# Fused attention and MLP on one Trainium2 core: one ScalarE Mish instruction in place of the exp, min, product, ln, exp chain

## The chip, the core and the metric

The kernel runs on one NeuronCore of a Trainium2 chip. A core has engines that run side by side and meet at semaphores: TensorE (PE, matrix multiply; its weight loads are listed as PEld), VectorE (DVE), ScalarE (ACT), GpSimd (POOL) and SyncE (SP, which issues most of the transfers). The metric is device time of one execution in microseconds (us). A lower time is better.

## What is computed

A relative-position attention whose output, laid out as 2304 tokens of 512 features, goes through an MLP with the Mish activation g = h * tanh(ln(1 + exp(h))). The first half is attention over 4 batches, 8 heads, 576 positions and 64 features a head, with a bias that a small network makes from the positions. The second half is where the change lies:

```python
def _moe_ref(x, w_in, w_out):          # x 2304 x 512, w_in 512 x 2048, w_out 2048 x 512
    h = x @ w_in
    sp = np.where(h > 20.0, h, np.log1p(np.exp(np.minimum(h, 20.0))))
    g = h * np.tanh(sp)
    return (g @ w_out).astype(np.float32)
```

## The kernel before

The program has three stages. The first (to about 60 us) makes the position bias and writes it out to memory (`evac`, L500 to L514). The second (to about 310 us) is attention: a software pipeline over 80 steps (`step`, L389), in which step n issues the scores of n, the exponentials of n, the transposes of n-2 on TensorE with their copies out of PSUM on ScalarE (L287, L290, L295, L296), and products with v (L313, L317). The last four steps, called with NS to NS+3, issue no exponentials any more: only transposes, copies and products.

The third stage is the MLP. The tokens are cut into five blocks (four of 512 and one of 256), and each block's hidden features into groups, which makes 72 units of one 128x512 tile each: 16 units for a block of 512 tokens, 8 for the block of 256. Every product is made of three fp32r matmuls (high x high, high x low, low x high parts) in order to keep fp32 accuracy, so a unit costs TensorE 12 matmuls of 512 columns in `hidden` (L581) and 12 in `project` (L615). In the block of 256 tokens `hidden` issues 24 of 256 columns instead.

The order of work is written by hand: each engine executes its instructions in the order of the program. In the loop at L669, round k issues `hidden` of unit k, `project` of unit k-3, and `gate` of unit k-1. So TensorE has two other unit-steps between the hidden product of a unit and its projection, plus one more of each kind. `hidden` writes h into one of four PSUM tiles. The rest of the activation is spread over two functions:

- `hidden`, after its matmuls: e = Exp(h) on ScalarE (L594), a minimum with E20 on VectorE (L595), and (e+2)*e on VectorE (L596). h stays in PSUM.
- `gate`: r = Ln(e+2) (L604) and r = Exp(-r) (L605) on ScalarE, which together make 1/(e+2); e = h*e (L606) and e = e*r (L607) on VectorE; then two splits of weights into high and low parts as long as any are left (`split_weights`, L130: a ScalarE copy at L135 and a VectorE subtraction at L136); then the split of the result: the high part as a ScalarE copy (L611) and the low part as a VectorE subtraction (L612).

`split_x` (L563) does the same for the next block's tokens (L570, L571, L573). The constant `two`, a tile of 128x96 of which one column is read, is the bias of the Ln. It is the first tile of the first pool on the left side of SBUF. At L49 the table set with both exp and ln is loaded on ScalarE before anything else. The units 0, 1 and 2 are begun between the attention's last steps (L652 to L660), so that the two stages overlap.

Of the kernel before, what the change touches and what calls it, by code (L numbers as in the profile page):

```python
# [7 lines left out]
F32 = mybir.dt.float32  # L8
F32R = mybir.dt.float32r
U32 = mybir.dt.uint32  # L10
AF = mybir.ActivationFunctionType
ALU = mybir.AluOpType
# [5 lines left out]
DM, DFF = 512, 2048  # L18
NT = B * S
P = 128  # L20
# [3 lines left out]
PAD = 16  # L24
PITCH = S + 2 * PAD
BIG = 3.0e38
E20 = 485165195.40979


ORDER = [0, 1, 4, 2, 3]  # L30
TB = 512
# [13 lines left out]
def kernel(ctx: ExitStack, tc, qk, v, wb, w2, w_in, w_out, psia, psi4, rinv, eye, out):  # L45
    nc = tc.nc
    pe, dve, act, pool, sp = nc.tensor, nc.vector, nc.scalar, nc.gpsimd, nc.sync
# [15 lines left out]
    const = sbuf("const")  # L63
# [4 lines left out]
    dram = ctx.enter_context(tc.tile_pool(name="dram", bufs=1, space=DRAM))  # L68


    two = const.tile([P, 96], F32, name="two")
    ident = const.tile([P, P], F32, name="ident")

    bias_d = [dram.tile([H, (P if c < 4 else 64) * PITCH + 2 * PAD], F32, name=f"bias_d{c}") for c in range(5)]
# [55 lines left out]
    def split_weights(eng):  # L130
        job, c = w32.pop(0)
        if job not in w_hi:
            w_hi[job] = ring.tile([P, 512], F32R, name="wh{}{}{}".format(*job))
            w_lo[job] = ring.tile([P, 512], F32R, name="wl{}{}{}".format(*job))
        act.copy(w_hi[job], c)  # L135
        eng.tensor_tensor(w_lo[job], c, w_hi[job].bitcast(F32), op=ALU.subtract)  # L136
# [317 lines left out]
    act.dma_start(out=psi4_t, in_=psi4)  # L454
    sp.dma_start(out=w2t, in_=w2)
    act.dma_start(out=rinv_t, in_=rinv)
    dve.memset(two, 2.0)
    dve.tensor_scalar(bb, psi4_t, wbt[:, 1:2], None, op0=ALU.mult)
    dve.tensor_scalar(at, at, wbt[:, 0:1], None, op0=ALU.mult)
    ts = [t for c in ORDER for t in range(8 * c, min(8 * c + 8, S // 16))]  # L460
    bps_t, h_t = {}, {}
# [14 lines left out]
    for idx, t in enumerate(ts):  # L476
# [4 lines left out]
        for cg in (3, 2, 1, 0):  # L481
            e = min(price, key=lambda k: spent[k] + price[k])
# [75 lines left out]
    mp = sbuf("mp", 2, side="right")  # L558
# [18 lines left out]
    h_t, gs, ys = {}, {}, {}  # L577
# [3 lines left out]
    def hidden(blk, fs):  # L581
        n = blocks[blk][1]
        h = h_ps.tile([P, TB], F32, name="h")
        for u, f in enumerate(fs):
            g4, r = divmod(f, 4)
            k = 0
            for w, x in ((w_hi, x_hi[blk]), (w_lo, x_hi[blk]), (w_hi, x_lo[blk])):
                for d in range(HP):
                    pe.matmul(h[:, u * n:(u + 1) * n], w["i", g4, d][:, r * P:(r + 1) * P], x[:, d, :n],  # L589
                              start=(k == 0), stop=(k == 11))  # L590
                    k += 1

        e = mp.tile([P, TB], F32, name="e", bufs=3)
        act.activation(e, h, AF.Exp)  # L594
        dve.tensor_scalar(e, e, E20, None, op0=ALU.min)  # L595
        dve.scalar_tensor_tensor(e, e, 2.0, e, op0=ALU.add, op1=ALU.mult)  # L596
        h_t[blk, fs] = (h, e)

    def gate(blk, fs, splits=0):
        r = mp.tile([P, TB], F32, name="r")  # L600
        ghi = mp.tile([P, TB], F32R, name="ghi")
        glo = mp.tile([P, TB], F32R, name="glo")
        h, e = h_t.pop((blk, fs))
        act.activation(r, e, AF.Ln, bias=two[:, 0:1])  # L604
        act.activation(r, r, AF.Exp, scale=-1.0)  # L605
        dve.tensor_tensor(e, h, e, op=ALU.mult)  # L606
        dve.tensor_tensor(e, e, r, op=ALU.mult)  # L607
        for _ in range(splits):
            if w32:
                split_weights(dve)  # L610
        act.copy(ghi, e)  # L611
        dve.tensor_tensor(glo, e, ghi.bitcast(F32), op=ALU.subtract)  # L612
        gs[blk, fs] = (ghi, glo)

    def project(blk, fs):  # L615
        t0, n = blocks[blk]
        ghi, glo = gs.pop((blk, fs))
        nt = n // P
        if fs[0] == 0:
            ys[blk] = [y_ps.tile([P, DM], F32, name=f"y{t}") for t in range(nt)]  # L620
        for t in range(nt):
            for u, f in enumerate(fs):
                g4, r = divmod(f, 4)
                whi, wlo = w_hi["o", g4, r], w_lo["o", g4, r]
                c0 = u * n + t * P
                for k, (g, w) in enumerate(((ghi, whi), (ghi, wlo), (glo, whi))):
                    pe.matmul(ys[blk][t], g[:, c0:c0 + P], w,  # L627
                              start=(f == 0 and k == 0), stop=(f == NFC - 1 and k == 2))
        if fs[-1] == NFC - 1:
            for t in range(nt):  # L630

                if t % 2 == 0:
                    yo = convp.tile([P, 512, 2], U32, name="w64").bitcast(F32).rearrange("p f t -> p (f t)")
                part = yo[:, t % 2 * DM:(t % 2 + 1) * DM]
                rows = out[t0 + t * P:t0 + (t + 1) * P, :]
                if blk == len(blocks) - 1 and t == nt - 1:

                    dve.tensor_copy(part[:, :DM // 2], ys[blk][t][:, :DM // 2])
                    rest = mp.tile([P, TB], F32, name="r")[:, :DM // 2]
                    act.copy(rest, ys[blk][t][:, DM // 2:])  # L640
                    sp.dma_start(out=rows[:, :DM // 2], in_=part[:, :DM // 2])
                    act.dma_start(out=rows[:, DM // 2:], in_=rest)
                    continue
                if t % 2:
                    act.copy(part, ys[blk][t])
                else:
                    dve.tensor_copy(part, ys[blk][t])
                sp.dma_start(out=rows, in_=part)
            del ys[blk]


    hidden(*units[0])  # L652
    step(NS)
    gate(*units[0])
    hidden(*units[1])
    step(NS + 1)
    gate(*units[1])
    hidden(*units[2])
    step(NS + 2)
    step(NS + 3)  # L660
# [8 lines left out]
    for k in range(2, len(units) + LAG2):  # L669
        if k < len(units):  # L670
            blk, fs = units[k]
            f = fs[0]
            if blk + 1 < len(blocks):
                early = 2 * (len(fs) - 1)
                if f == 6 - 2 * early:
                    load_x(blk + 1, xp)
                    x_lo[blk + 1] = (xa if blk % 2 else xp).tile([P, HP, TB], F32R, name="xlo")
                    load_r(blk + 1, x_lo[blk + 1].bitcast(F32), 0, HP)

                if f >= 8 - early:  # L680
                    split_x(blk + 1, XPARTS[f - 8 + early:f - 8 + early + len(fs)])
            if k > 2:
                hidden(blk, fs)
        if k >= LAG2:
            project(*units[k - LAG2])
        if 2 <= k - 1 < len(units):
            gate(*units[k - 1], 2)
# [54 lines left out]
```

## Time and profile before

| | us |
|---|---|
| median of three runs | 701.82 (701.07 to 703.33) |
| span of the profiled execution | 700.9 |
| TensorE matmul busy | 672.9 (96%) |
| VectorE busy | 517.3 (74%) |
| ScalarE busy | 458.4 (65%) |
| GpSimd busy | 72.4 (10%) |
| mean granted TensorE clock | 0.994 of full speed |

The page cuts the span into 40 slices. TensorE shows a 9 in tenths in every slice from the seventh to the last but one. VectorE and ScalarE fall from 8 and 9 in the attention to 5 to 7 and 4 to 5 in the MLP. A share of busy time is a mean over stages with different limits, so the views below are read stage by stage. A row of the chain of waits says at which time which piece of work held the end of the program; a row of the waits says who waited for whom.

### The profile page before, as it was taken

The page shows a single profiled execution, that of the slowest core. Times are in us where ns is not written, and L with a number is a line of the kernel's source. Part 1 is how long each engine was busy: PE and PEld are TensorE (multiplying, and loading weights), DVE is VectorE, ACT ScalarE, POOL GpSimd, SP SyncE. Part 2 cuts the span into 40 slices and gives each one's busy share as a digit, 9 for nine tenths or more (in the row PEclk, how much of TensorE's full clock was granted, in tenths as well). Part 3 has the DMA queues.
Part 4 walks back from the last instruction along what each step waited for, and adds up shares of the span by engine and source line. Part 5 has one row for each costly group of instructions (what it writes and reads, how often), then busy time and mean ns, then how long its engine had stood idle before and what let it go on. Part 6 is the DMA issues. An engine that isn't in the chain of part 4 may idle for free.

```text
span 700.9 us, 13630 instructions
## 1 busy us (share of the span) xinstructions
PE 672.9 (96%) x5156; PEld 511.2 (73%) x5156; DVE 517.3 (74%) x1082; ACT 458.4 (65%) x987; POOL 72.4 (10%) x85
## 2 busy tenths in 40 slices
PE   5878999999999999999999999999999999999997
PEld 2224666776777666668888888889988888888886
DVE  7995898888988878868788566655775567665554
ACT  6895988888899888876675544444554455454443
POOL 0000142322222222710000000000000000000000
PEclk9999999999999999999999999999999999999999
DMA  4997688787778767204000120023005000010001
GB/s 150 318 285 228 195 273 263 216 284 225 245 234 266 241 231 240 55 22 116 1 1 0 66 56 1 1 76 106 1 1 150 1 1 0 1 60 1 1 0 60
DMA packets 46081, 81.88 MB, mean 117 GB/s; under 512 B 14400, under 2 KB 23104, under 8 KB 46016
## 3 DMA queue, kind: packets, MB, share of 16 engines
q1 hardware_dynamic: 43568, 72.70, 32.8%
q0 software_dynamic: 1872, 8.09, 3.9%
q8 instruction: 40, 0.66, 0.4%
q10 hardware_dynamic: 576, 0.22, 0.1%
q14 instruction: 25, 0.20, 0.1%
HBM read 60.60 MB, written 20.40 MB: 116 GB/s over the span
## 4 chain that ended last, share of the span: by engine, by line
PE 71%; ACT 9%; DVE 7%; DMA 3%; issue 2%; DVEq 0%; ACTq 0%
PE h L589 28%; PE y L627 28%; PE o L313 5%; PE s L220 5%; ACT pt L252 5%; DVE pt L237 4%; ACT main L295 3%; PE tp L287 3%; PE tp L290 1%; DMA w<-in_w_in_dram 1%; DMA w<-in_w_out_dram 1%; PE o L317 1%; DVE w L123 1%; DVE x L320 1%; DVE w L125 1%
## 5 line engine op out<-in xcount | busy, mean ns | idle before, releaser
L252 ACT ACTIVATE pt<-pt,m 128x576 f32<-128x576 f32 x144 | 112.2, 780 | 33.5 <-DVE m L237 32.9
L627 PE MATMUL y<-who,ghi 128*128 128x512 f32 x288 | 112.1, 389 | 0.0
L627 PE MATMUL y<-wlo,ghi 128*128 128x512 f32 x288 | 112.1, 389 | 0.0
L627 PE MATMUL y<-who,glo 128*128 128x512 f32 x288 | 112.0, 389 | 0.0
L611 ACT CAST ghi<-e 128x512 fp32r<-128x512 f32 x72 | 44.7, 621 | 93.5 <-DVE e L607 93.5
L237 DVE CUSTOM_DVE_ANT_0 pt<-s,bias 128x576 f32<-128x576 f32 (+1 forms) x112 | 81.3, 753 | 17.8 <-PE s L220 16.6
L594 ACT ACTIVATE e<-h 128x512 f32<-128x512 f32 x72 | 43.0, 597 | 65.9 <-PE h L589 65.7
L595 DVE TENSOR_SCALAR e<-e 128x512 f32<-128x512 f32 x72 | 30.6, 426 | 74.0 <-ACT e L594 74.0
L612 DVE TENSOR_TENSOR glo<-e,ghi 128x512 fp32r<-128x512 f32 x72 | 49.8, 692 | 44.9 <-ACT ghi L611 44.9
L589 PE MATMUL h<-xhi,whi 128*128 128x512 f32 (+1 forms) x320 | 79.1, 369 | 0.0
L589 PE MATMUL h<-xhi,wli 128*128 128x512 f32 (+1 forms) x320 | 78.7, 368 | 0.0
L589 PE MATMUL h<-xlo,whi 128*128 128x512 f32 (+1 forms) x320 | 78.7, 368 | 0.0
L313 PE MATMUL o<-main,vt 128*64 128x320 f32 (+1 forms) x512 | 73.8, 411 | 3.1 <-DVE x L320 3.0
L295 ACT COPY main<-tp 128x512 f32<-128x512 f32 x126 | 66.5, 577 | 2.0 <-DMA bias_d<-bt 1.9
L287 PE MATMUL tp<-ident,pt 64*128 64x64 f32 x1184 | 61.7, 227 | 6.3 <-ACT main L295 4.7
L589 PEld LDWEIGHTS h<-xhi,whi 128*128 128x128 f32 x320 | 57.1, 188 | 11.7 <-issue 0.7
L287 PEld LDWEIGHTS tp<-ident,pt 64*128 64x128 f32 x1184 | 53.5, 139 | 15.2 <-ACT main L295 13.1
L589 PEld LDWEIGHTS h<-xhi,wli 128*128 128x128 f32 x320 | 56.9, 189 | 10.0
L589 PEld LDWEIGHTS h<-xlo,whi 128*128 128x128 f32 x320 | 56.9, 189 | 10.0
L627 PEld LDWEIGHTS y<-who,glo 128*128 128x128 f32 x288 | 54.1, 188 | 11.3
L627 PEld LDWEIGHTS y<-who,ghi 128*128 128x128 f32 x288 | 54.1, 188 | 11.0
L627 PEld LDWEIGHTS y<-wlo,ghi 128*128 128x128 f32 x288 | 54.1, 188 | 10.9
(69 smaller groups left out, 1126.9 us busy)
## 6 DMA issues: line engine op xcount, KB each, us to landing
bias_d<-bt SPq DMA_DIRECT2D x36, 295.5 KB
w<-in_w_in_dram SPq DMA_DIRECT2D x16, 512.0 KB
w<-in_w_out_dram SPq DMA_DIRECT2D x16, 512.0 KB
qkhi<-in_qk_dram POOLq DMA_DIRECT2D x13, 608.0 KB, 4.5
rawqk<-in_qk_dram SPq DMA_DIRECT2D x13, 608.0 KB
vt<-in_v_dram SPq DMA_DIRECT2D x16, 320.0 KB
out_dram<-w SPq DMA_DIRECT2D x17, 256.0 KB
x_d<-x SPq DMA_DIRECT2D x32, 128.0 KB
```

The source lines that it names most:

```text
L220: pe.matmul(s[:, j, :SH], q[rows, c * P:(c + 1) * P], k[rows, KO + j * SH:KO + (j + 1) * SH], start=(t == 0), stop=(t == len(terms) - 1))
L237: dve.tensor_tensor_reduce(out=halves(pt[rows, sl]), in0=s[rows, :, :SH], in1=halves(bt[rows, sl]), scale=-0.125, scalar=BIG, op0=ALU.add, ...
L252: act.activation(ps, ps, AF.Exp, bias=m[:, u:u + 1], scale=-1.0, accum_out=sums[i][:, k:k + 1])
L287: pe.transpose(tp[:, k * 64:k * 64 + 64], pt[rows, c0:c0 + P], ident[rows, rows])
L295: copy(main[:, :, :, q0:q0 + 64], tp.rearrange("p (h k q) -> p h k q", h=2, k=4))
L313: pe.matmul(o[h * 64:h * 64 + 64, :w], vt[:, h, k, :], main[:, h, k, :], start=(k == 0), stop=False, **kw)
L589: pe.matmul(h[:, u * n:(u + 1) * n], w["i", g4, d][:, r * P:(r + 1) * P], x[:, d, :n], start=(k == 0), stop=(k == 11))
L594: act.activation(e, h, AF.Exp)
L595: dve.tensor_scalar(e, e, E20, None, op0=ALU.min)
L611: act.copy(ghi, e)
L612: dve.tensor_tensor(glo, e, ghi.bitcast(F32), op=ALU.subtract)
L627: pe.matmul(ys[blk][t], g[:, c0:c0 + P], w, start=(f == 0 and k == 0), stop=(f == NFC - 1 and k == 2))
```

## The change

`hidden` ends with its matmuls. `gate` has one ScalarE instruction with the Mish function, which reads h from PSUM and writes g to SBUF, and then the splits as before. The tile e (three buffers) and the constant `two` with its memset are gone; r (two buffers) is now called g. The preload at L49 is left as it is.

```diff
-    two = const.tile([P, 96], F32, name="two")
...
-    dve.memset(two, 2.0)
...
-        e = mp.tile([P, TB], F32, name="e", bufs=3)
-        act.activation(e, h, AF.Exp)
-        dve.tensor_scalar(e, e, E20, None, op0=ALU.min)
-        dve.scalar_tensor_tensor(e, e, 2.0, e, op0=ALU.add, op1=ALU.mult)
-        h_t[blk, fs] = (h, e)
+        h_t[blk, fs] = h
 
     def gate(blk, fs, splits=0):
-        r = mp.tile([P, TB], F32, name="r")
+        g = mp.tile([P, TB], F32, name="g")
         ghi = mp.tile([P, TB], F32R, name="ghi")
         glo = mp.tile([P, TB], F32R, name="glo")
-        h, e = h_t.pop((blk, fs))
-        act.activation(r, e, AF.Ln, bias=two[:, 0:1])
-        act.activation(r, r, AF.Exp, scale=-1.0)
-        dve.tensor_tensor(e, h, e, op=ALU.mult)
-        dve.tensor_tensor(e, e, r, op=ALU.mult)
+        act.activation(g, h_t.pop((blk, fs)), AF.Mish)
         for _ in range(splits):
             if w32:
                 split_weights(dve)
-        act.copy(ghi, e)
-        dve.tensor_tensor(glo, e, ghi.bitcast(F32), op=ALU.subtract)
+        act.copy(ghi, g)
+        dve.tensor_tensor(glo, g, ghi.bitcast(F32), op=ALU.subtract)
         gs[blk, fs] = (ghi, glo)
...
-                    rest = mp.tile([P, TB], F32, name="r")[:, :DM // 2]
+                    rest = mp.tile([P, TB], F32, name="g")[:, :DM // 2]
```

## Rows read from the trace of the kernel before

**Rows 1.** Chain of waits, hand-over and MLP: start us, us, engine, tile, line, count

```profile
292.45 0.70 PE tp L287 x15
...
302.14 2.99 PE h L589 x12
...
314.88 2.72 PE y L627 x12
...
686.24 10.21 PE y L627 x45
```

**Rows 2.** Windows: span, then busy us (instructions) of PE PEld DVE ACT POOL, clock, DMA

```profile
40.00:60.00 20.00, 15.41 (x150) 5.61 (x144) 16.45 (x43) 14.82 (x36) 0.18 (x2) 0.98 0.91 284
340.00:360.00 20.00, 20.00 (x90) 16.57 (x89) 16.02 (x27) 12.62 (x22) 0.00 (x0) 1.00 0.00 0
```

**Rows 3.** Waits of PE from 285 to 372 us: total us, times, longest

```profile
PE tp L287 <- ACT main L295: 0.4, 2, 0.2
```

**Rows 4.** Lines by form, 340 us on: count | busy us, mean ns | idle before, releaser

```profile
L604 ACT ACTIVATE r<-e,two 128x512 f32<-128x512 f32 x65 | 46.5, 715 | 0.0
L607 DVE TENSOR_TENSOR e<-e,r 128x512 f32<-128x512 f32 x65 | 45.0, 692 | 7.1 <-DVE e L606 0.5
L606 DVE TENSOR_TENSOR e<-h,e 128x512 f32<-128x512 f32 x65 | 44.4, 684 | 4.5 <-ACT r L604 4.5
L596 DVE SCALAR_TENSOR_TENSOR e<-e 128x512 f32<-128x512 f32 x64 | 44.3, 693 | 2.2
L605 ACT ACTIVATE r<-r 128x512 f32<-128x512 f32 x65 | 41.3, 635 | 2.1
L611 ACT CAST ghi<-e 128x512 fp32r<-128x512 f32 x66 | 41.0, 621 | 89.5 <-DVE e L607 89.5
L594 ACT ACTIVATE e<-h 128x512 f32<-128x512 f32 x64 | 38.2, 597 | 58.0 <-PE h L589 57.8
L595 DVE TENSOR_SCALAR e<-e 128x512 f32<-128x512 f32 x64 | 27.2, 426 | 66.6 <-ACT e L594 66.6
...
L571 ACT CAST xhi<-xraw 128x512 fp32r<-128x512 f32 x12 | 7.4, 621 | 15.1 <-DVE xraw L570 15.1
...
L135 ACT CAST who<-w 128x512 fp32r<-128x512 f32 x8 | 4.6, 610 | 0.0
```

**Rows 5.** ACT timeline at the start: the table load before the first function

```profile
0.74 1.28 ACT L49 ACT_TABLE_LOAD   x1 [0.74 <-PEq L729]
```

**Rows 6.** ACT timeline at the hand-over: start us, us, line, operation [idle before]

```profile
301.47 0.28 ACT L296 COPY tail<-tp 128x128 f32<-128x128 f32 x1
...
305.16 0.60 ACT L594 ACTIVATE e<-h 128x512 f32<-128x512 f32 x1 [0.50 <-PE h L589]
305.81 1.08 ACT L295 COPY main<-tp 128x512 f32<-128x512 f32 x2
```

**Rows 7.** PE timeline at the hand-over

```profile
305.06 0.71 PE L287 MATMUL tp<-ident,pt 64*128 64x64 f32 x16
...
309.01 2.37 PE L313 MATMUL o<-main,vt 128*64 128x320 f32 x16
```

**Rows 8.** ACT timeline at the end

```profile
695.80 0.59 ACT L645 COPY w<-y 128x512 f32<-128x512 f32 x1 [2.77 <-PE y L627]
697.61 0.37 ACT L640 COPY r<-y 128x256 f32<-128x256 f32 x1 [1.23 <-DVE w L638]
```

**Rows 9.** DVE timeline at the end

```profile
695.12 0.69 DVE L647 COPY w<-y 128x512 f32<-128x512 f32 x1 [1.37 <-PE y L627]
```

**Rows 10.** PE timeline at the end

```profile
693.78 0.39 PE L627 MATMUL y<-wlo,ghi 128*128 128x512 f32 x1
...
695.14 0.39 PE L627 MATMUL y<-wlo,ghi 128*128 128x512 f32 x1
```

**Rows 11.** Chain of waits at the end of the bias stage

```profile
54.43 4.05 DMA bias_d<-bt
```

More of the change, by code (lines that the diff above doesn't have):

```diff
@@ L26 @@
 BIG = 3.0e38
-E20 = 485165195.40979
 ORDER = [0, 1, 4, 2, 3]
```

## The prediction, made before the changed kernel ran

> **What bounds the kernel now.** I read the chain of waits first, because it says which work held the end at each moment. From 292.45 us on every piece of it is TensorE's, one behind the other without a gap: transposes and products of the last attention steps, the first hidden products between them (the longest, 2.99 us), and from 314.88 us the steady pattern, in which a hidden product and a projection take 2.72 us each, 5.44 us a unit. The last piece, 10.21 us of projections, ends at 686.24 + 10.21 = 696.45 us [rows 1]. The windows say the same in another way: from 340 to 360 us TensorE is busy for 20.00 of 20.00 us at full granted clock, while VectorE has 16.02 and ScalarE 12.62 [rows 2]. The waits of TensorE itself settle it: between 285 and 372 us it waited 0.4 us in all, for copies of the attention's transposes, and for nothing that the activation makes [rows 3]. The two engines that the change relieves do wait, and a lot: the copy of the high part waits 89.5 us in all for the product before it, the first Exp 58.0 us for TensorE, the minimum 66.6 us for that Exp [rows 4]. These are waits of engines with time to spare.
>
> **What the change removes.** Per unit, from the rows of the steady stage [rows 4]: on VectorE 0.426 + 0.693 + 0.684 + 0.692 = 2.495 us (minimum, sum and product, two products), on ScalarE 0.597 + 0.715 + 0.635 = 1.947 us (Exp, Ln, Exp). Over 72 units that is 180 us of VectorE and 140 us of ScalarE. None of it lies on the path: TensorE doesn't wait for it. Worth at the end: 0. The memset of the constant at the start goes too; its result is first read by the Ln in the MLP, so this is 0 as well.
>
> **What it adds.** One ScalarE instruction per unit, of a function that the trace of before doesn't show. The nearest row is the Exp that reads the same h from PSUM in the same shape with no pointer operand, 0.597 us; the Ln with a pointer to its bias takes 0.715 us [rows 4]. I take 0.60 us. From the other side, I bound it by what ScalarE can hide: after the change a unit with everything in it has one high-part copy (0.621), two weight copies (2 x 0.610) and one token copy (0.621), 2.46 us, out of TensorE's 5.44 us; the Mish instruction could take 2.98 us, five times the Exp, before ScalarE became the bound [rows 1, 4]. With 0.60 us ScalarE needs 3.06 us of the 5.44, and most units, which have no weights or tokens left to split, 1.22 us. Cost: 0, between 0 and 0 up to five times the row.
>
> **One table load more.** The preload names a set with exp and ln. If Mish is in another, ScalarE has to load a table once, since after the attention's last Exp nothing but copies and Mish is left. The row of a load is 1.28 us [rows 5]. Behind it on ScalarE stand the first Mish, its copy, and the copies of the next transposes, for which TensorE's products wait. The cover: ScalarE ends the copies of step NS at 301.47 + 0.28 = 301.75 us. Load 1.28, Mish 0.60 and high-part copy 0.62 end at about 304.25 us. The next copies started at 305.81 us before, behind an Exp that itself waited for h (the change removes that Exp from here), and their transposes only start at 305.06 and last 0.71 us [rows 6, 7]. So about 1.5 us of cover is left in front of these copies, and behind them another 309.01 - 306.89 = 2.1 us until the products that read them [rows 6, 7]. A load of up to some 4.9 us would be free. Without the cover it would cost its own 1.28 us, once, 0.2%. Cost taken: 0, bounds 0 and 1.3 us.
>
> [...]
>
> **What moves.** ScalarE no longer waits for a new h in the middle of the round; it reads h one round later, in `gate`. So h stays in PSUM no longer than before, when the product h*e read it there in the same function: the four buffers suffice. The waits of the high-part copy for VectorE (89.5 us) go, and ScalarE waits for TensorE instead: nothing is late next, as the Mish of unit k-1 needs an h that is a round old. No transfer is issued in `hidden` or `gate`, so no queue is moved past.
>
> **The end.** Behind TensorE's last matmul stand VectorE's copies, ScalarE's copy at 697.61 us and the transfer of the result [rows 8]. None is touched but for the name of a tile. Cost 0.
>
> **Sum.** 700.9 us of span + 0 = 700.9 us. The median of the runs, 701.82 us, stands 0.9 us above the span; I carry this over and forecast 701.8 us. About 0.3%, 2.1 us, is what a measurement of this kernel can tell from no change; its own three runs spread over 2.3 us.
>
> **Rivals.**
>
> *TensorE was held back by the other engines all along.* [...] The end of the trace speaks against it: VectorE was idle for 1.37 us before 695.12 us and ScalarE for 2.77 us before 695.80 [rows 8, 9], and in that stretch six matmuls took 695.14 - 693.78 = 1.36 us [rows 10], 0.227 us each, the pace of the busy stretch to the digit. Chance 0.02. A small form of it: the four hidden products in the hand-over take up to 2.99 us instead of 2.72 [rows 1]; all of that back is at most 1.1 us, 700.7, inside the bound of no change.
>
> *The addresses move (slower, or faster).* The constant taken out is 384 bytes per partition at the head of the left side of SBUF; every tile of bias and attention on that side moves by as much. The one place where transfers hold the end for long is the write-out of the bias: the transfer engines are busy for 0.91 of 40 to 60 us [rows 2], and a piece of 4.05 us at 54.43 us is on the chain [rows 11]. If transfers from the new addresses are slower there, the piece grows; I price it at its own length, twice it or none: 705.9 us or 697.8. It decides from 2.1 us on, about 5% over the 40 us in which the bias is written out. No row shows a transfer at two alignments, so I can't exclude it. Chance 0.04 for each sign.
>
> [...]
>
> *The tables are swapped in every unit (slower).* If the copies of the MLP needed another set than Mish, each unit would have two loads: 2 x 1.28 + 0.60 + 0.62 = 3.8 us, or 5.0 us with the two weight copies, still under 5.44; only units with a token copy too reach 5.6 us [rows 1, 4, 5], which makes some 2 us over a dozen such units: 704 us. It hurts from 2.1 us a load on, (5.44 - 1.22) / 2; every 0.1 us above that costs 72 x 0.2 = 14 us. Against it: in the row of before the copies are COPY and CAST operations, not ACTIVATE, and run in one set beside Exp and Ln [rows 4]. Chance 0.04.
>
> [...]
>
> *The change doesn't do what it says:* Mish is made of several instructions. Up to 2.98 us a unit this gives the same time, 701.8. Chance 0.03, and it is counted as no change.
>
> **How the numbers follow.** The forecast has 0.83, with noise of a measurement 0.02 of that on either side outside 0.3%. Faster: 0.02 (contention) + 0.04 (addresses) + 0.02 (noise) = 0.08. Slower: 0.04 + 0.04 + 0.02 = 0.10, of which some of the table case is hidden: 0.08. No change: 0.84. The range takes the noise of the three runs on either side, and the bound of the table load, 1.3 us: 699.8 to 703.9 us. It leaves the address cases and the contention out, which hold about 0.1, and the far half of the table case.
>
> **What would show it.** Right: TensorE's pieces from 292 us on stand without a gap at 2.72 us; one more table load of about 1.3 us at about 300 to 302 us; Mish at about 0.60 us; VectorE's busy time about 180 us lower, ScalarE's about 97 us (140 - 72 x 0.60); the last matmul at about 696.5 us. Wrong: TensorE waiting for ghi, glo or a copy at L295 after 300 us, a matmul pace other than 0.227 us, table loads in more than one place, or the first score of the attention and the bias write-out ending more than 1 us away from before.

## The result, and the profile after

The changed kernel takes 710.13 us (median of four runs, 709.19 to 711.09) where the kernel before takes 701.93: a ratio of 1.0107, 95% interval 1.0083 to 1.0132. It is slower by 8.2 us. The forecast was no change at 701.8 us.

| | before | after |
|---|---|---|
| span of the profiled execution, us | 700.9 | 708.2 |
| TensorE busy, us | 672.9 | 681.8 |
| VectorE busy, us | 517.3 | 346.9 |
| ScalarE busy, us | 458.4 | 365.2 |
| mean granted TensorE clock | 0.994 | 0.993 |

The relief came as forecast: VectorE works 170 us less and ScalarE 93 us less. But TensorE, which has the same 5156 matmuls to do, is busy 8.9 us longer. The chain of waits of the changed kernel (start us, us, engine, tile, line, count) shows where; its rows answer to [rows 1]:

```profile
295.11 2.94 PE h L586 x12
...
315.86 2.80 PE h L586 x12
...
380.18 2.80 PE y L616 x12
382.98 2.73 PE h L586 x12
...
693.10 10.52 PE y L616 x45
```

There is still no gap in it, and 12 matmuls take 2.80 us instead of 2.72: 0.233 us a matmul instead of 0.227. In the kernel before, the first hidden product starts at

```profile
296.91 2.92 PE h L589 x12
```

and the last projection ends at 696.45 us [rows 1], 399.5 us later. After, it is from 295.11 to 693.10 + 10.52 = 703.62 us, 408.5 us. So the MLP takes 9.0 us more. It starts 1.8 us sooner, and what follows the last matmul takes 0.1 us more: 9.0 - 1.8 + 0.1 = 7.3 us of span. Of the remaining 0.9 us of the 8.2, 0.8 lies outside the span (709.94 us for the execution whose span is 708.2, 701.82 for 700.9), a part that ranges from 1.7 to 2.9 us within the runs of the first experiment below alone; so the experiments are compared by their ratios and by the length of the MLP.

The windows exclude a slower clock, and VectorE or ScalarE being short of time. The columns are those of [rows 2]; TensorE is busy 20.00 of 20.00 us at full granted clock, in 88 matmuls instead of 90, while VectorE and ScalarE are busy for no more than 3.37 and 3.98 us of the later stretch:

```profile
340.00:360.00 20.00, 20.00 (x88) 16.09 (x87) 9.10 (x15) 10.44 (x19) 0.00 (x0) 1.00 0.00 0
600.00:620.00 20.00, 20.00 (x88) 16.27 (x87) 3.37 (x5) 3.98 (x7) 0.00 (x0) 1.00 0.00 1
```

The lines by form from 340 us on answer to [rows 4]. The Mish instruction takes 593 ns, and ScalarE now runs so far ahead that the copy of the high part waits for TensorE to free its buffer:

```profile
L600 ACT CAST ghi<-g 128x512 fp32r<-128x512 f32 x65 | 40.4, 621 | 231.7 <-PE y L616 231.6
L596 ACT ACTIVATE g<-h 128x512 f32<-128x512 f32 x65 | 38.6, 593 | 0.0
```

And the ScalarE timeline at the hand-over shows the one table load, which answers to [rows 5, 6]:

```profile
299.69 0.28 ACT L294 COPY tail<-tp 128x128 f32<-128x128 f32 x1
299.99 1.28 ACT L596 ACT_TABLE_LOAD   x1
301.29 0.60 ACT L596 ACTIVATE g<-h 128x512 f32<-128x512 f32 x1
301.92 0.62 ACT L600 CAST ghi<-g 128x512 fp32r<-128x512 f32 x1
303.99 1.08 ACT L293 COPY main<-tp 128x512 f32<-128x512 f32 x2 [1.45 <-PE tp L285]
```

### The profile page after: what moved, and what is told of

Same layout as the page of the kernel before. It is cut to its first block, busy times and chain, and to the rows that moved or that the text cites. A ratio compares the mean times of both kernels' runs of the same rounds, so it can differ in the third digit from the quotient of the medians.

```text
span 708.2 us, 13125 instructions
## 1 busy us (share of the span) xinstructions
PE 681.8 (96%) x5156; PEld 510.5 (72%) x5156; DVE 346.9 (49%) x793; ACT 365.2 (52%) x844; POOL 72.1 (10%) x85
## 4 chain that ended last, share of the span: by engine, by line
PE 75%; DVE 10%; ACT 10%; issue 3%; DMA 2%; DVEq 0%; ACTq 0%
PE h L586 28%; PE y L616 28%; PE s L218 5%; PE o L311 5%; ACT pt L250 4%; DVE pt L235 4%; ACT main L293 3%; PE tp L285 3%; PE bps L524 3%; DVE ht L494 2%; PE tp L288 1%; DMA vt<-in_v_dram 1%; DVE w L121 1%; PE o L315 1%; DVE w L123 1%
## 5 line engine op out<-in xcount | busy, mean ns | idle before, releaser
L601 DVE TENSOR_TENSOR glo<-g,ghi 128x512 fp32r<-128x512 f32 x72 | 49.9, 693 | 287.3 <-ACT ghi L600 287.3
L600 ACT CAST ghi<-g 128x512 fp32r<-128x512 f32 x72 | 44.7, 621 | 249.0 <-PE y L616 248.8
L616 PE MATMUL y<-who,glo 128*128 128x512 f32 x288 | 113.7, 395 | 0.0
L616 PE MATMUL y<-wlo,ghi 128*128 128x512 f32 x288 | 113.7, 395 | 0.0
L616 PE MATMUL y<-who,ghi 128*128 128x512 f32 x288 | 113.6, 394 | 0.0
L168 POOL TENSOR_TENSOR qklo<-rawqk,qkhi 128x304 fp32r<-128x304 f32 x52 | 46.1, 911 | 124.9 <-DMA rawqk<-in_qk_dram 124.9
L524 PE MATMUL bps<-ht,w2t 128*32 128x512 f32 (+17 forms) x352 | 38.8, 560 | 14.3 <-ACT bt L506 6.1
```

The lines of the kernel that those rows point to most:

```text
L168: pool.tensor_tensor(lo[:, sl], raw[:, sl], hi[:, sl].bitcast(F32), op=ALU.subtract)
L524: pe.matmul(ps[cg * 32:cg * 32 + 32, a:min(a + 512, n)], w2t, h_t[idx, cg][:, a:min(a + 512, n)], start=True, stop=True)
L600: act.copy(ghi, g)
L601: dve.tensor_tensor(glo, g, ghi.bitcast(F32), op=ALU.subtract)
L616: pe.matmul(ys[blk][t], g[:, c0:c0 + P], w, start=(f == 0 and k == 0), stop=(f == NFC - 1 and k == 2))
```

## The experiments

What else changed than the instructions? The tile `two` stood at the head of the left side of SBUF, 384 bytes a partition. By the addresses that the program allots, before the change all weights, tokens and split results of the MLP start at a multiple of 512 bytes. After it, the weights in the pools `ring` and `wq` on the left have moved by 384 bytes and start 128 bytes past one; the tokens, ghi, glo and the first four input weights (pool `weights`), on the right, have not moved. The first four hidden products of a block use those first four weights, and they are the ones at 2.73 us in the chain above (382.98 us).

Three theories. P: TensorE is slower on operands that start off a grid. R: it is slower where the two operands of its work, the weights it loads and the tile it streams, are off a grid with regard to each other. T: the new timing, with ScalarE and VectorE writing ghi and glo as soon as TensorE frees them, slows its reads.

**The place given back.** A filler tile that nobody uses stands where the constant stood:

```diff
+    const.tile([P, 96], F32, name="pad")
     ident = const.tile([P, P], F32, name="ident")
```

> The changed kernel with a tile of 384 bytes a partition, which nobody reads or writes, where the constant stood, so that every tile of the left side stands at its old address. Theory P (placement: TensorE is slower on weights that were moved by 384 bytes): 12 matmuls of 512 columns take 2.72 us again, the last matmul ends near 695 us, 700 to 702 us in all. Theory T (timing: ScalarE and VectorE, now ahead, write ghi and glo as soon as TensorE frees them and slow its reads): 2.80 us, 710 us, as in the changed kernel.

Measured: ratio to the kernel before 0.9994 (0.9970 to 1.0019). The chain:

```profile
295.64 2.94 PE h L587 x12
...
359.83 2.72 PE h L587 x12
362.55 2.72 PE y L617 x12
...
692.89 2.28 PE y L617 x10
```

The MLP takes 399.5 us from first hidden product to last matmul (692.89 + 2.28 = 695.17 us), as before. The one Mish instruction is all there, at 593 ns, and from 340 us on VectorE's instructions add up to 78.2 us where they add up to 241.5 in the kernel before. T has fallen, and the Mish instruction itself costs and brings nothing that can be measured.

**The old chain, moved.** The other way round: the kernel before, its constant wider by 128 bytes.

```diff
-    two = const.tile([P, 96], F32, name="two")
+    two = const.tile([P, 128], F32, name="two")
```

> The kernel before with its whole chain, but its constant tile is 128 columns wide instead of 96, so that the left side moves by 128 bytes and its tiles start 128 bytes past a multiple of 512, as in the changed kernel. Theory P: 2.80 us per 12 matmuls and about 9 us more in the MLP, 709 to 712 us. Theory T: 2.72 us and 701.9 us, as the chain is the old one.

Measured: ratio 1.0141 (1.0111 to 1.0171), and an MLP of 408.5 us, as in the changed kernel:

```profile
296.56 2.94 PE h L589 x12
...
362.06 2.80 PE h L589 x12
364.85 2.80 PE y L627 x12
...
694.55 10.52 PE y L627 x45
```

32 more columns in a tile of which one is read make the MLP of the old kernel longer by as much as the whole change did; the ratios of the two kernels, 1.0141 and 1.0107, have overlapping intervals. The slowdown is the placement's.

**Both sides moved.** The changed kernel with the right side moved by 128 bytes too, by a filler tile that stands there already:

```diff
-    sbuf("edge", side="right").tile([P, 120], F32, name="edge")
+    sbuf("edge", side="right").tile([P, 88], F32, name="edge")
```

> The changed kernel with the right side of SBUF (tokens, ghi, glo, first weights) moved by 128 bytes too, by a narrower filler tile, so that both operands of every matmul of the MLP start 128 bytes past a multiple of 512. Theory P in its absolute form: at least 2.80 us per 12 matmuls everywhere, the first four units of a block too, 710 us or more. Theory R (only the distance between the two operands of a matmul counts): 2.72 us and 702 us. Theory T: 2.80 us, 710 us.

Measured: ratio 0.9997 (0.9978 to 1.0016).

```profile
360.72 2.72 PE h L586 x12
363.44 2.72 PE y L616 x12
```

No operand of the MLP starts at a multiple of 256 bytes here, and the pace is the fast one. P in its absolute form has fallen: R holds.

**The right side alone.** The filler of the first experiment and the narrower `edge` of the third.

> The changed kernel with the left side at its old addresses and the right side moved by 128 bytes. In project the weights stream and the split g is loaded, in hidden the tokens stream and the weights are loaded. Theory P, if what streams must start on the grid: hidden 2.80, project 2.72 us. If what is loaded must: hidden 2.72 us but for the first four units of a block (their weights stand on the right), project 2.80. If either spoils it: both at 2.80, 710 us. Theory R: both at 2.80 but for the first four hidden units of a block at 2.72, about 709 us. Theory T: 2.80 everywhere.

Measured: ratio 1.0107 (1.0078 to 1.0136), 2.80 us for hidden and project, but 2.73 us for the first four hidden products of a block of 512 (in the changed kernel 2.74 for the one that stands behind the block of 256), whose weights moved together with the tokens:

```profile
380.87 2.80 PE y L617 x12
383.67 2.73 PE h L587 x12
```

It is the changed kernel's pattern from the other side, as R expects. I had expected 2.72 us for those four; the experiment with a part of the weights put back comes back to them.

**How wide the grid is.** Fillers of other widths in the first experiment's place: 32, 112 and 104 columns, then 16, 120 and 8, so that weights and right side are 256, 64, 32, 192, 96 and 160 bytes apart on a grid of 512.

> The changed kernel with a filler of 128 bytes, so that the left side stands 256 bytes past a multiple of 512 and the right side on one: the two operands of a matmul are 256 bytes apart on a grid of 512. Theory R with a grid of 512: 2.80 us per 12 matmuls, 710 us. Theory R with a grid of 256 or less: 2.72 us, 702 us.

> The changed kernel with a filler of 448 bytes: the left side stands 64 bytes past a multiple of 512, the right side on one. Theory R with a grid of 128 or more: a pace other than 2.72 us, 2.80 us if every distance off the grid costs the same, 710 us. With a grid of 64 or less: 2.72 us, 702 us. Below 2.72 us is open too: no row so far shows a distance between 0 and 128.

> The changed kernel with a filler of 416 bytes: the left side stands 32 bytes past a multiple of 512, the right side on one. Theory R: between 2.72 and 2.80 us per 12 matmuls if the cost grows with the distance, 2.80 us if every distance off the grid costs the same; 702 to 710 us.

> The changed kernel with a filler of 64 bytes: left side 192 bytes past a multiple of 256, right side on one. Theory R with a grid of 256 bytes where every other distance costs: 2.76 to 2.80 us per 12 matmuls of 512 columns, as at 64 bytes. If the sign of the distance counts: below that, perhaps below 2.72 us, which no distance so far gives.

> The changed kernel with a filler of 480 bytes: left side 96 bytes past a multiple of 256, right side on one. Theory R with a grid of 256 bytes: 2.76 to 2.80 us per 12 matmuls of 512 columns. A pace under 2.72 us would show that zero is not the best distance.

> The changed kernel with a filler of 32 bytes: left side 160 bytes past a multiple of 256, right side on one. Theory R with a grid of 256 bytes: 2.76 to 2.80 us per 12 matmuls of 512 columns. A pace under 2.72 us would show that zero is not the best distance.

The three first have ratios of 1.0013 (0.9988 to 1.0038), 1.0097 (1.0067 to 1.0128) and 1.0155 (1.0098 to 1.0212); the three others, run once each, took 712.32, 713.77 and 712.94 us, where the kernel before had a median of 703.35 in the same series. The chains, in the order of 256, 64, 32, 192, 96 and 160 bytes:

```profile
362.02 2.72 PE h L587 x12
364.74 2.72 PE y L617 x12
```

```profile
362.87 2.79 PE y L617 x12
365.66 2.80 PE h L587 x12
368.46 2.76 PE y L617 x12
```

```profile
362.36 2.80 PE y L617 x12
365.15 2.80 PE h L587 x12
```

```profile
362.59 2.79 PE h L587 x12
365.38 2.80 PE y L617 x12
368.19 2.76 PE h L587 x12
```

```profile
363.51 2.79 PE h L587 x12
366.30 2.81 PE y L617 x12
```

```profile
362.52 2.81 PE h L587 x12
365.33 2.81 PE y L617 x12
```

Of the eight distances tried, 0 and 256 bytes give 2.72 us, and 32, 64, 96, 128, 160 and 192 give 2.76 to 2.81. A grid of 256 bytes fits these eight, and 512 bytes does not; that other multiples of 256 behave alike was not shown. None of the eight is better than 0 for matmuls of 512 columns. The cost doesn't grow with the distance, but it isn't the same everywhere: at 64 bytes the projections and at 192 the hidden products go at 2.76 and 2.80 us in turn. From the first hidden product to the last matmul of their chains the MLP takes 399.5 us at 0 and 256 bytes, 406.7 at 64, 407.9 at 192, 408.5 at 128, 409.2 at 32, 409.4 at 160 and 409.6 at 96.

**A part of the weights put back.** Only the weights in `wq` are put back at their old distance; those in the ring stay moved.

```diff
     wq = sbuf("wq")
+    wq.tile([P, 96], F32, name="pad")
```

> The changed kernel with 384 bytes of filler at the head of the pool wq alone: the weights in wq (input groups 1 and 2, output pieces 0 to 6) are at the old distance from tokens and ghi, those in the ring (input group 3, output pieces 7 to 15) stay moved. Theory R on these operands: in a block of 512 tokens hidden units 0 to 11 at about 2.72 us and 12 to 15 at 2.80, projections 0 to 6 at 2.72 and 7 to 15 at 2.80; in all about 56 slow groups instead of 120, 4.3 us over the aligned kernel, 705.5 to 707 us. If something else on the left side makes the pace (attention's leftovers, the layout of the ring's waits): no such pattern by unit.

Measured: ratio 1.0060 (1.0034 to 1.0085), an MLP of 403.9 us, 4.3 over 399.5, which was the number expected. The chain from project unit 6 and hidden unit 10 of the second block on:

```profile
296.56 2.94 PE h L586 x12
...
435.25 2.72 PE y L616 x12
437.96 2.72 PE h L586 x12
440.69 2.79 PE y L616 x12
443.48 2.73 PE h L586 x12
...
449.00 2.80 PE h L586 x12
...
689.92 10.52 PE y L616 x45
```

The pace changes unit by unit with the pool of the weights: projections slow from unit 7 on, hidden products from unit 12 on. Nothing else changes at these places, so it is these operands and no other tile of the left side. Hidden unit 11 (443.48 us) shows one thing more: its own weights are at distance 0 from its tokens, yet it takes 2.73 us. It comes right behind a slow projection, while hidden unit 10 comes behind a fast one. The timeline puts the loss into its first four matmuls, which take 0.93 us, where the next four take 0.90 and the last four 0.91:

```profile
443.31 1.08 PE L586 MATMUL h<-xhi,whi 128*128 128x512 f32 x4
444.24 1.07 PE L586 MATMUL h<-xhi,wli 128*128 128x512 f32 x4
445.14 1.07 PE L586 MATMUL h<-xlo,whi 128*128 128x512 f32 x4
446.05 0.40 PE L616 MATMUL y<-who,ghi 128*128 128x512 f32 x1
```

The first four hidden products of a block in the changed kernel stand behind slow projections in the same way and take 2.73 us as well. So in both kernels a group at distance 0 took 0.01 us more behind a slow group. In the changed kernel the weights of such a group are loaded from 382.59 us on, while the last matmul of the projection before still streams:

```profile
382.59 0.39 PE L616 MATMUL y<-who,glo 128*128 128x512 f32 x1
382.59 0.88 PEld L586 LDWEIGHTS h<-xhi,whi 128*128 128x128 f32 x4
```

Whether the loss comes from this overlap was not shown. Nor is it 0.01 us everywhere: in the kernel with a distance of 64 bytes one of the first four hidden products of a block takes 2.77 us, 0.05 more:

```profile
385.12 2.76 PE y L617 x12
387.88 2.77 PE h L587 x12
```

**The short block.** At 64 bytes the hidden products of the block of 256 tokens were faster than at 0, 2.74 and 2.75 us for 24 matmuls where the first experiment has 2.87:

```profile
482.79 2.74 PE h L587 x24
```

So the left side was left in its old place, and only that block's tokens moved within their tiles:

```diff
+    x0s = [0, 0, 48, 0, 0]
...
-    pe.matmul(h[:, u * n:(u + 1) * n], w["i", g4, d][:, r * P:(r + 1) * P], x[:, d, :n],
+    pe.matmul(h[:, u * n:(u + 1) * n], w["i", g4, d][:, r * P:(r + 1) * P], x[:, d, x0s[blk]:x0s[blk] + n],
```

(and likewise where these columns are loaded and split).

> The changed kernel with the left side at its old addresses, and only the tokens of the block of 256 moved within their tiles by 48 columns, 192 bytes, so that in that block's hidden products weights and tokens are 64 bytes apart. In the kernel with a distance of 64 bytes the 24 matmuls of 256 columns took 2.74 to 2.75 us where they take 2.87 at distance 0. Theory R: 2.72 us everywhere else, about 2.75 us in the eight hidden products of this block, 1.0 us less than with the left side at its old addresses alone: ratio to the kernel before 0.997 to 1.001. Otherwise 2.87 us there, and no gain.

Measured: ratio 0.9997 (0.9981 to 1.0014). The hidden products of this block take 2.83 us, not 2.75, where they took 2.87 with the filler alone, and the projections between them 2.72 instead of 2.75:

```profile
468.39 2.83 PE h L589 x24
471.21 2.72 PE y L619 x12
```

8 x (0.04 + 0.03) = 0.6 us: the MLP is that much shorter in the trace (399.0 us for 399.5), but the time of a run can't tell it from nothing. No kernel tried beats the one before by more than the noise.

Why it is not 2.75 us stays open, but another trace has the same figure. Weights 64 bytes past the tokens and tokens 192 bytes past the weights are the same distance only on a signed grid of 256. With the weights 192 bytes past the tokens, the 24 matmuls, from the third hidden product of the block on, take 2.83 us too:

```profile
485.38 2.83 PE h L587 x24
```

So for matmuls of 256 columns these two runs go by the 192 bytes, whichever tile is ahead; that the distance counts with a sign and modulo 256 bytes is not shown for them.

## Why the prediction was wrong

*What bounds the kernel* was right: TensorE, without a gap, before and after [rows 1]. It is also why the error shows in full: between 340 and 360 us TensorE was busy for 20.00 of 20.00 us before and after, so the 9.0 us of the MLP had no cover.

*What the change removes* was right in mechanism and near in size: 170 us of VectorE instead of 180, 93 us of ScalarE instead of 97, and worth nothing at the end, as the experiment with the place given back shows (0.9994).

*What it adds*: the Mish instruction at 593 ns for 0.60 forecast. *One table load more* was right: 1.28 us as in [rows 5], once, right behind the copies of step NS, and the next copies wait for the transposes afterwards for 1.45 us, the cover that was worked out as 1.5. The copy before ends at 299.97 us, the load runs from 299.99 to 301.27, and Mish starts at 301.29.

*The step that failed* is the one about the constant: "The memset of the constant at the start goes too; its result is first read by the Ln in the MLP, so this is 0 as well." It counted what the constant does and not the room that it takes, and so the sum had no term for TensorE's pace. That term measures 9.0 us: 4 x 12 hidden products and 72 projections, 120 groups of 12 matmuls, which take 2.80 us instead of 2.72, or 9.0 / 120 = 0.075 us more each on the average.

*The rival "the addresses move"* had the right cause, 384 bytes, in the wrong place and at the wrong price. I looked for its price where transfers hold the end, and gave it 4.05 us and a chance of 0.04. The write-out of the bias didn't grow: its last piece on the chain ends at 58.48 us before [rows 11], and after it is this:

```profile
55.73 3.22 DMA bias_d<-bt
```

which ends at 58.95 us. It was also no test of alignment on the grid of 256 bytes that the matmuls suggest: by the addresses that the program allots, the 36 pieces start 0, 64, 128 and 192 bytes past a multiple of 256, nine pieces each, before the change and after it; the 384 bytes only change which piece starts where. Whether transfers depend on such a grid was not shown. The loss arose in the matmuls of the MLP; between 340 and 360 us, where their pace is the slow one, the transfer engines' busy share is 0.00. The prediction names the tiles of bias and attention as moved; that the MLP's weights stand on the same side, and that TensorE reads them beside tiles of the right side, which stay, it left out.

*The rival of contention* asked the right question with too narrow a comparison. That six matmuls at the end took 0.227 us each beside idle engines [rows 8 to 10] speaks against VectorE and ScalarE slowing TensorE, and the first experiment bears it out: 2.72 us as before, with 78.2 us of VectorE's instructions from 340 us on instead of 241.5. The forecast gives contention a chance of 0.02 to make the kernel faster; no run shows 12 matmuls of 512 columns in less than 2.72 us, and so none shows a gain from it. From the six matmuls I took the pace for a constant. But every matmul of the MLP in the trace of before had its operands at distance 0, so the trace couldn't show what another distance costs: a constant in a trace is only constant under the conditions that the trace contains. By the prediction's own mark ("a matmul pace other than 0.227 us") the profile told so at once.

*The start of the MLP* is 1.8 us sooner after (295.11 for 296.91 us), before the first Mish instruction has run. Over the other kernels it lies between 293.98 and 297.85 us, also where the placement is that of before (295.64 with the filler of 96 columns). I take it for the attention's own variation between executions; it was not tested.

What stays open: why the distance of 128 bytes costs about 0.006 us a matmul (9.0 us over 1440) and the other five tried about as much, how far a slow group reaches into the next, and why matmuls of 256 columns behave otherwise. The runs show when it happens and how much it costs, not the mechanism.

## What to carry to other kernels

Before a buffer is removed or resized, list which tiles move with it, and whether the engine that bounds the kernel reads any of them: here 384 bytes moved the weights, and the MLP took 9.0 us more. When that engine has no idle time and still takes longer, compare the pace of one instruction of one shape before and after; then give the old place back with a filler before suspecting the new instructions. Taking work off engines that wait was worth nothing at the end here (0.9994 with the old place given back).

## What the runs showed of the hardware that was not expected

All of it was measured in the kernels of this document, on one core, at a mean granted clock of 0.992 to 0.998 of full speed in the profiled executions. Twelve fp32r matmuls of 512 columns took 2.72 us where the tile that TensorE loads as weights and the tile that it streams are 0 bytes apart on a grid of 512 (the kernel before, and the changed kernel with the place given back) or 256 bytes apart (the filler of 32 columns). They took 2.79 or 2.80 us at 128 bytes (the changed kernel, and the old chain moved), 2.80 at 32, 2.76 to 2.80 at 64 and at 192, and 2.79 to 2.81 at 96 and at 160. Between 340 and 360 us of the changed kernel the granted clock was 1.00 and TensorE busy for 20.00 of 20.00 us, so it is neither the clock nor a wait. In these runs it is the distance and not the place itself: with both sides moved by 128 bytes the pace was 2.72 us and the ratio 0.9997. A group at distance 0 behind a slow one took 2.73 us in the changed kernel and 2.77 in the one with 64 bytes.

For the hidden products of 256 columns the order was another one: 24 took 2.87 us at distance 0 (the place given back), 2.74 and 2.75 with the weights 64 bytes past the tokens, and 2.83 with a distance of 192 bytes, whether the weights (the filler of 16 columns) or the tokens (the short block) are ahead. No run shows the mechanism.
